# Sign bits' products moved to even turns, weights' steps spread over five, row sums six wide

## The chip, the cores and the metric

The kernel runs on one core of a Trainium2 chip. The metric is device time in microseconds; three runs of the kernel before gave 622.32 as the median (620.95 to 622.4). Five engines work at once, each through its own instructions in order: TensorE (PE; its weight loads are shown as PEld), VectorE (DVE), ScalarE (ACT), GpSimd (POOL), and SyncE (SP), which here only issues transfers.

## What is computed

Attention in which a query sees only keys of the same hash bucket, then a gated feed-forward layer. The reference, shortened:

```python
q_bits = (einsum('bhsd,dk->bhsk', q, proj) > 0)      # 6 sign bits; the same for k
mask = q_bucket[:, :, :, None] == k_bucket[:, :, None, :]
scores = where(mask, scale * q @ k.T, -1e9)
attn = softmax(scores);  x = attn @ v                # 4 batches, 8 heads, 768 tokens, 64 wide
gate = sigmoid(causal 5-tap convolution of x)        # x: 4 x 768 x 512
out = (gate * (x @ w_val)) @ w_out
```

The weights arrive as float64 and are split into a high and a low float32 part.

## The kernel before, in words

There are 32 heads (`units`), each with six tiles of 128 queries, so 192 turns of one loop over `k` (L514). A pipeline runs through the turns. Turn `k` copies the transposed probabilities of tile k - 4 out of PSUM (ScalarE, L348), takes the row maximum of tile k (VectorE, L297), forms its factor and shift (L303, L307), issues the scores of tile k + 1 (TensorE, L291) and the exponentials of tile k (ScalarE, L315), and ends with the transposes of tile k - 3 (TensorE, L339). On even turns the row sums of two tiles are taken (`row_sums`, L321, and `recip`, L325); GpSimd scales the probabilities by them (L330). On odd turns the product with the values follows (`av`, L362).

Between these, generators are stepped, each step issuing a little work: `preps` makes the next head's stacked operands (copies and a difference on GpSimd, L195 and L198, then transfers on SP, L199 to L207); `convs` the convolution (four of five taps on VectorE, L393); `moes` the feed-forward; `weights` the splitting of the eight weight tiles, of six turns each; `ahead` the sign bits of heads 16 to 31.

**Sign bits.** The mask is made by adding rows to the score matmul: twelve rows of sign bits stand below the 64 rows of each operand. For four heads at once, `bits` (L221) or `early_bits` (L236) multiplies half of their rows by `proj_sb` into one PSUM bank (four small matmuls, called a product below), and VectorE turns it into bits by a comparison (L232, L254). Products and comparisons are issued in one step, one behind the other. The bits of heads 0 to 15 come from `bits`, whose operands `raws` are the heads' whole inputs, five buffers; for heads 4 to 15 it runs at the end of the `prep` of the head before. Those of heads 16 to 31 come from `early_bits`, in turns 9 to 57 with k % 6 equal to 3 or 4; its rows are loaded apart, into the feed-forward's `hh` and `hl` buffers (five each), and the bits are stored to memory (`ud`).

**The bank.** The pool `ps_m` has one bank, `m`. The feed-forward's sums use it from turn 65 on, the products and, in `split_weight` (L105), the weights before that: a weight tile holds it from the absolute value on ScalarE (L111) to the last of the operations on VectorE that read it (L121).

**What sets the order.** On TensorE, VectorE, ScalarE and GpSimd the program's order is the order of execution. SP's queue is ordered by the planner of the framework, which places a transfer when its data and its buffer are ready by its own estimate; the queue is then in order too, and a transfer that waits holds those behind it. Waits are inserted from the tiles' accesses.

Of the kernel before, what the change touches and what calls it, by code (L numbers as in the profile page):

```python
# [8 lines left out]
FP32 = mybir.dt.float32  # L9
FP32R = mybir.dt.float32r  # L10
AF = mybir.ActivationFunctionType
ALU = mybir.AluOpType
# [14 lines left out]
def kernel(  # L27
# [77 lines left out]
    def split_weight(w, hi, lo, fetch):  # L105
        if w.dtype == I32:

            t = ps_m.tile([P, 512], FP32, name="m")
            l, u = w[:, :, 0], w[:, :, 1]
            a, d, ti = u.bitcast(FP32), l.bitcast(FP32), t.bitcast(I32)  # L110
            nc.scalar.activation(out=t, in_=a, func=AF.Abs)  # L111
            yield
            nc.vector.tensor_scalar(out=t, in0=t, scalar1=LEAST, scalar2=None, op0=ALU.max)
            nc.vector.tensor_scalar(out=ti, in0=ti, scalar1=3, scalar2=0x3fffffff,
                                    op0=ALU.logical_shift_left, op1=ALU.bitwise_and)
            yield
            fetch()
            nc.vector.scalar_tensor_tensor(out=u, in0=u, scalar=-2 ** 30, in1=ti,
                                           op0=ALU.bitwise_and, op1=ALU.bitwise_or)
            nc.vector.tensor_scalar(out=ti, in0=u, scalar1=-2 ** 23, scalar2=None, op0=ALU.bitwise_and)  # L120
            nc.vector.scalar_tensor_tensor(out=d, in0=l.bitcast(U32), scalar=2.0 ** -52, in1=t,  # L121
                                           op0=ALU.mult, op1=ALU.mult)
            yield
            nc.vector.tensor_copy(out=hi, in_=a)
            nc.gpsimd.tensor_tensor(out=a, in0=a, in1=hi.bitcast(FP32), op=ALU.subtract)
            nc.gpsimd.tensor_tensor(out=lo, in0=a, in1=d, op=ALU.add)
        else:
            nc.scalar.copy(out=hi, in_=w)
            yield
            yield  # L130
            fetch()
            yield
            nc.gpsimd.tensor_tensor(out=lo, in0=w, in1=hi.bitcast(FP32), op=ALU.subtract)
# [52 lines left out]
    def prep(i):  # L186

        if i >= len(units):
            return
        b, h = units[i]  # L190
        j = h % 4
        load_values(i)
        r = raws[i]
        aq, ak, bq, bk = stacks[i] = [stk.tile([P, S], FP32R, name=nm) for nm in ("aq", "ak", "bq", "bk")]
        nc.gpsimd.tensor_copy(out=aq, in_=r)  # L195
        if i > 1:
            yield
        nc.gpsimd.tensor_tensor(out=bq, in0=r, in1=aq.bitcast(FP32), op=ALU.subtract)  # L198
        nc.sync.dma_start(out=ak[0:D].bitcast(FP32), in_=aq[D:P].bitcast(FP32))  # L199
        nc.sync.dma_start(out=bk[0:D].bitcast(FP32), in_=aq[D:P].bitcast(FP32))  # L200
        nc.sync.dma_start(out=bk[D:P].bitcast(FP32), in_=bq[D:P].bitcast(FP32))
        nc.sync.dma_start(out=bq[D:P].bitcast(FP32), in_=aq[0:D].bitcast(FP32))
        if i == 1:
            yield
        u = cur["u"]
        nc.sync.dma_start(out=aq[D:M].bitcast(FP32), in_=f32(u[32 * j:32 * j + 2 * NB]))
        nc.sync.dma_start(out=ak[D:M].bitcast(FP32), in_=f32(u[32 * j + 2 * NB:32 * j + 4 * NB]))  # L207
        load_raw(i + 5)
        if j == 3 and i + 1 < len(units):
            if i + 1 in early:  # L210
                cur["u"] = early.pop(i + 1)
            else:
                yield
                yield from bits(i + 1)

    def side_tile():
        if not moes:
            return ps_m.tile([P, 512], FP32, name="m")
        return ps_t.tile([P, 512], FP32, name="tp")

    def bits(i):  # L221

        u = stk.tile([P, S], FP32R, name="u", bufs=2)
        for hf in range(2):
            yield
            sl = slice(hf * HS, (hf + 1) * HS)
            z = side_tile()
            for jj in range(4):
                nc.tensor.matmul(out=z[32 * jj:32 * jj + 32, 0:HS], lhsT=proj_sb,  # L229
                                 rhs=raws[i + jj][:, sl], start=True, stop=True,  # L230
                                 tile_position=(0, 32 * jj))
            nc.vector.tensor_scalar(out=u[:, sl], in0=z[:, 0:HS], scalar1=rows_sb[:, 0:1], scalar2=rows_sb[:, 1:2],  # L232
                                    op0=ALU.is_ge, op1=ALU.mult)
        cur["u"] = u

    def early_bits():  # L236

        for i in range(16, len(units), 4):
            u = dram.tile([P, S], FP32, name="ud")
            rows = []  # L240
            for hf, name in enumerate(("hh", "hl")):
                yield
                rows.append([hp.tile([P, HS], FP32R, name=name).bitcast(FP32) for _ in range(4)])
                for jj, t in enumerate(rows[-1]):
                    b, h = units[i + jj]
                    nc.sync.dma_start(out=t, in_=qk[b, h, :, hf * HS:(hf + 1) * HS])
            for hf in range(2):
                yield
                z = ps_m.tile([P, 512], FP32, name="m")
                for jj, t in enumerate(rows[hf]):  # L250
                    nc.tensor.matmul(out=z[32 * jj:32 * jj + 32, 0:HS], lhsT=proj_sb, rhs=t, start=True, stop=True,
                                     tile_position=(0, 32 * jj))
                t = hp.tile([P, HS], FP32, name="ht", bufs=2)
                nc.vector.tensor_scalar(out=t.bitcast(FP32R), in0=z[:, 0:HS], scalar1=rows_sb[:, 0:1],  # L254
                                        scalar2=rows_sb[:, 1:2], op0=ALU.is_ge, op1=ALU.mult)
                nc.sync.dma_start(out=u[:, hf * HS:(hf + 1) * HS], in_=t)
            early[i] = u

    def first_bits():
        yield from bits(0)  # L260
        load_raw(5)

    def first_prep():
# [53 lines left out]


    def row_sums(k):
        sums[k] = small.tile([P, 2, 2], FP32, name="s1")  # L320
        nc.vector.tensor_scalar(out=sums[k][:, :, 0], in0=ps[k][1][:, :, 0], scalar1=1e-9, scalar2=None, op0=ALU.add)  # L321

    def recip(k):
        ri = small.tile([P, 2], FP32, name="ri")
        nc.vector.reciprocal(out=ri, in_=sums.pop(k)[:, :, 0])  # L325
        rcs[k], rcs[k + 1] = ri[:, 0:1], ri[:, 1:2]

    def normalise(k):
# [152 lines left out]
    tiles = [(i, qt) for i in range(len(units)) for qt in range(KB)]  # L481

    raws, stacks, vts, ss, nbs, ps, tps, sums, rcs, nms, gs, cur = {}, {}, {}, {}, {}, {}, {}, {}, {}, {}, {}, {}
    avs, convs, moes, early = [], [], [], {}
    accs = [(ps_m, "m")]

    def step(gens):

        while gens:
            try:  # L490
                return next(gens[0])
            except StopIteration:
                gens.pop(0)
# [7 lines left out]
    with tc.manual_schedule(engines=ENGINES):  # L501
# [9 lines left out]
        step(weights[0])  # L511
        step(weights[1])
        ahead = [early_bits()]
        for k in range(N + LAG + 1):  # L514
            if 0 <= k - LAG - 1:
                keep_transposed(k - LAG - 1)
            pair = k % 2 == 0 and 0 <= k - 2 < N
            if k < N:
                maxima(k)
            if pair:  # L520
                row_sums(k - 2)
            if k < N:
                factors(k)
            if pair:
                recip(k - 2)
            if 0 <= k - 2 < N:
                normalise(k - 2)
            if k < N:
                shifts(k)
            if k + 1 < N:  # L530
                if tiles[k + 1][0] != tiles[k][0]:
                    finish(preps)
                    preps = [prep(tiles[k + 1][0] + 1)]
                scores(k + 1)
            if k < N:
                exponentials(k)
            if k >= 60 or k % 2:
                step(convs)
            if k % 6 in (0, 2, 4, 5) and k > 4:
                step(weights[0])  # L540
            elif k < 6:
                step(weights[1])

            thin = k // 6 % 8 in (7, 0) and k < 186
            for _ in range(3 if cur["gates"] else (1, 0)[k % 2] if thin else 1):
                step(moes)
            cur["gates"] = max(0, cur["gates"] - 1)
            step(preps)
            if 6 <= k < 60 and k % 6 in (3, 4):
                step(ahead)  # L550
            if k % 2:
                step(avs)
                step(avs)
            if 0 <= k - LAG < N:
                transposes(k - LAG)
# [67 lines left out]
```

## Time and profile before

| | |
|---|---|
| median of 3 runs | 622.32 us (620.95 to 622.4) |
| the profiled execution | 621.24 us, span 619.2 us |
| TensorE busy | 585.0 us, 94% of the span |
| VectorE busy | 434.5 us, 70% |
| ScalarE busy | 420.3 us, 68% |
| GpSimd busy | 387.6 us, 63% |
| granted TensorE clock | 0.997 |

Times in the views are microseconds from the start of the span. In a row of the timeline come start, duration, engine, line, operation, out<-in, shapes and count, and in brackets how long the engine was idle before it and what released it. In a row of a stretch come its bounds and length, then busy time and count for each engine that took part, the granted clock, the share of the transfer engines and GB/s. Matmul ends are modelled, so a busy TensorE isn't TensorE at its peak.

### The profile page before, as it was taken

To read this page: it belongs to the slowest core of one execution; us is meant where nothing else is said; L and a number is where in the kernel's file an instruction comes from. 1 tells how busy PE (TensorE), PEld (TensorE's weight loads), DVE (VectorE), ACT (ScalarE), POOL (GpSimd) and SP (SyncE) were. 2 spreads that over 40 slices of the span, in tenths; PEclk is the share of its full clock that TensorE was granted. 3 is DMA by queue.
4 is the path that set the end of the run, shared out by engine and by line. 5 is a ranking of instruction groups with operands and counts; after the bars stand their busy time and mean duration, and the time that the engine had idled before them with its cause. 6 is when DMAs were issued, how large, how long until landed. Compare 5 with 4: busy or idle time off the path is not lost.

```text
span 619.2 us, 10665 instructions
## 1 busy us (share of the span) xinstructions
PE 585.0 (94%) x3496; PEld 421.4 (68%) x3496; DVE 434.5 (70%) x1017; ACT 420.3 (68%) x881; POOL 387.6 (63%) x373
## 2 busy tenths in 40 slices
PE   5799998989899999999999999999999999999997
PEld 2665655556567776776668787777667777775895
DVE  5787889898885866668575867668665877665532
ACT  2786777677778676777787676777787766765400
POOL 3575777677866765578665777468764776544321
PEclk9899999999999999999999999999999999999999
DMA  7575767473533334243434234333422213200111
GB/s 228 167 209 168 216 170 208 129 202 82 132 82 74 79 77 130 73 108 83 125 80 115 55 83 123 87 112 83 108 70 78 68 43 92 66 19 1 51 52 51
DMA packets 29030, 64.64 MB, mean 104 GB/s; under 512 B 4936, under 2 KB 10056, under 8 KB 28976
## 3 DMA queue, kind: packets, MB, share of 16 engines
q1 hardware_dynamic: 28832, 63.93, 37.7%
q8 instruction: 28, 0.46, 0.3%
q14 instruction: 26, 0.21, 0.1%
q10 hardware_dynamic: 144, 0.03, 0.0%
HBM read 30.60 MB, written 7.86 MB: 62 GB/s over the span
## 4 chain that ended last, share of the span: by engine, by line
PE 71%; ACT 14%; DVE 11%; issue 2%; DMA 2%; SPq 0%; POOL 0%; ACTq 0%; DVEq 0%; POOLq 0%
PE av L362 19%; PE s L291 17%; PE tp L339 13%; PE m L449 8%; PE m L424 7%; ACT p L315 6%; ACT pt L348 4%; DVE nm L297 3%; ACT x L370 2%; DVE g L393 2%; PE tp L424 1%; PE tp L449 1%; PE s L449 1%; PE m L229 1%; PE s L424 1%
## 5 line engine op out<-in xcount | busy, mean ns | idle before, releaser
L330 POOL TENSOR_SCALAR p<-p,ri 128x768 f32<-128x768 f32 x192 | 205.0, 1072 | 157.7 <-DVE nb L307 131.3
L297 DVE TENSOR_REDUCE nm<-s 128x1 f32<-128x768 f32 x192 | 182.6, 951 | 63.9 <-PE s L291 63.5
L348 ACT COPY pt<-tp 128x384 f32<-128x384 f32 x384 | 165.7, 485 | 81.7 <-PE tp L339 80.9
L315 ACT ACTIVATE p<-s,nb,gs 128x768 f32<-128x768 f32 x192 | 192.7, 1003 | 40.5 <-DVE nb L307 35.6
L339 PEld LDWEIGHTS tp<-ident,p 128*128 128x128 f32 x1152 | 129.2, 141 | 71.8 <-issue 45.2
L339 PE MATMUL tp<-ident,p 128*128 128x128 f32 x1152 | 163.8, 278 | 2.8 <-ACT pt L348 2.2
L362 PE MATMUL av<-pt,vt 128*64 128x384 f32 x768 | 144.9, 498 | 0.0
L291 PE MATMUL s<-ak,aq 76*128 76x384 f32 x384 | 117.7, 387 | 19.6 <-ACT p L315 16.9
L291 PE MATMUL s<-bk,bq 128*128 128x384 f32 x384 | 100.6, 343 | 0.4 <-DVE bq L277 0.4
L362 PEld LDWEIGHTS av<-pt,vt 128*64 128x64 f32 x768 | 46.9, 136 | 63.0 <-issue 62.9
L291 PEld LDWEIGHTS s<-ak,aq 76*128 76x128 f32 x384 | 59.0, 193 | 35.6 <-ACT p L315 31.8
L393 DVE SCALAR_TENSOR_TENSOR g<-x,cw_sb,g 128x768 f32<-128x768 f32 x64 | 77.3, 1208 | 2.2 <-POOL g L391 2.1
L291 PEld LDWEIGHTS s<-bk,bq 128*128 128x128 f32 x384 | 71.2, 192 | 0.8 <-issue 0.8
L198 POOL TENSOR_TENSOR bq<-r,aq 128x768 fp32r<-128x768 f32 x31 | 57.5, 1853 | 0.1
L435 POOL TENSOR_TENSOR hl<-ht,hh 128x384 fp32r<-128x384 f32 x32 | 32.2, 1006 | 39.4 <-DVE hh L433 39.4
L370 ACT COPY x<-av 64x384 f32<-64x384 f32 x64 | 30.4, 474 | 30.9 <-PE av L362 30.2
L383 POOL TENSOR_TENSOR xl<-x,xh 128x384 fp32r<-128x384 f32 x32 | 33.4, 1059 | 18.0 <-DVE xh L382 18.0
L424 PE MATMUL m<-xh,wv 128*128 128x384 f32 x200 | 42.7, 337 | 0.0
L307 DVE TENSOR_SCALAR nb<-nm,gs 128x1 f32<-128x1 f32 x192 | 40.2, 209 | 3.5
L315 ACT ACTIVATION_READ_ACCUMULATOR p<-s,nb,gs 128x1 f32 x192 | 39.1, 203 | 0.0
L429 DVE TENSOR_TENSOR ht<-m,g 128x384 f32<-128x384 f32 x25 | 13.9, 556 | 35.7 <-PE m L424 29.3
L449 PE MATMUL m<-wo,hh 128*128 128x512 f32 x144 | 38.1, 394 | 0.0
(86 smaller groups left out, 483.7 us busy)
## 6 DMA issues: line engine op xcount, KB each, us to landing
r<-in_qk_dram SPq DMA_DIRECT2D x32, 384.0 KB
vt<-in_v_dram SPq DMA_DIRECT2D x16, 384.0 KB
out_dram<-o SPq DMA_DIRECT2D x24, 256.0 KB
ak<-aq SPq DMA_DIRECT2D x31, 192.0 KB
bk<-aq SPq DMA_DIRECT2D x31, 192.0 KB
bk<-bq SPq DMA_DIRECT2D x31, 192.0 KB
bq<-aq SPq DMA_DIRECT2D x31, 192.0 KB
hh<-in_qk_dram SPq DMA_DIRECT2D x16, 192.0 KB
```

Of the source, the lines that this page charges most:

```text
L198: nc.gpsimd.tensor_tensor(out=bq, in0=r, in1=aq.bitcast(FP32), op=ALU.subtract)
L291: nc.tensor.matmul(out=s[:, hf, 0:HS], lhsT=lq[0:n, qs], rhs=rk[0:n, hf * HS:(hf + 1) * HS], start=n == M, stop=n == P)
L297: nc.vector.tensor_reduce(out=nm, in_=s[:, :, 0:HS], axis=AX.XY, op=ALU.max, negate=True)
L315: nc.scalar.activation(out=p, in_=s[:, :, 0:HS], func=AF.Exp, bias=nb, scale=gs.pop(k), accum_out=sm[:, k % 2, 0:1])
L330: nc.gpsimd.tensor_scalar(out=p, in0=p, scalar1=rcs.pop(k), scalar2=1.0, op0=ALU.mult, op1=ALU.mult)
L339: nc.tensor.transpose(out=tp[:, n * P:(n + 1) * P], in_=p[:, kb * P:(kb + 1) * P], identity=ident)
L348: nc.scalar.copy(out=pt[:, :, qo:qo + P], in_=tp[:, 0:HS].rearrange("p (a b) -> p a b", b=P))
L362: nc.tensor.matmul(out=av[s * D:(s + 1) * D, 0:HS], lhsT=vt[:, kb, hh * D:(hh + 1) * D], rhs=pt[kb // 3][:, kb % 3, :], start=(kb == 0), s ...
L370: nc.scalar.copy(out=x[hh * D:(hh + 1) * D, o:o + HS], in_=av[s * D:(s + 1) * D, 0:HS])
L393: nc.vector.scalar_tensor_tensor(out=g, in0=x[:, k:k + S], scalar=w, in1=g, op0=ALU.mult, op1=ALU.add)
L424: nc.tensor.matmul(out=acc[:, 0:HS], lhsT=wv[wi][:, c, j * P:(j + 1) * P], rhs=xs_[(c, o)][xi], start=(m == 0), stop=(m == 11))
L449: nc.tensor.matmul(out=acc, lhsT=hs[(o, j)][hi][:, tb * P:(tb + 1) * P], rhs=wo[wi][:, j, :], start=(m == 0), stop=(m == 11))
```

## The change

The products get turns written out by hand (`marks`), all even and, up to turn 52, the fifth of six; the comparison (`signs`) follows one turn later, behind that turn's exponentials. All use the bank `m`; `side_tile` goes. `bits` for heads 4, 8 and 12 no longer hangs on `prep` but is a generator of its own. `early_bits` loads both halves of its first group in one step at turn 8, and each half of the next group right behind the comparison of that half. The weights' steps come at the end of a turn, after the products, and in five turns of six (not the fourth); the first of the three operations that followed the fetch (L118) gets a step of its own ahead of it. The row sums are written three times over, as six columns, and the reciprocal reads the first two.

```diff
@@ split_weight
             yield
-            fetch()
             nc.vector.scalar_tensor_tensor(out=u, in0=u, scalar=-2 ** 30, in1=ti,
                                            op0=ALU.bitwise_and, op1=ALU.bitwise_or)
+            yield
+            fetch()
             nc.vector.tensor_scalar(out=ti, in0=u, scalar1=-2 ** 23, scalar2=None, op0=ALU.bitwise_and)
@@ prep
+        if j == 0:
+            cur["u"] = us.pop(i)
         u = cur["u"]
...
         load_raw(i + 5)
-        if j == 3 and i + 1 < len(units):
-            if i + 1 in early:
-                cur["u"] = early.pop(i + 1)
-            else:
-                yield
-                yield from bits(i + 1)
+    def product(rows):
+        z = ps_m.tile([P, 512], FP32, name="m")
+        for jj, t in enumerate(rows):
+            nc.tensor.matmul(out=z[32 * jj:32 * jj + 32, 0:HS], lhsT=proj_sb, rhs=t, start=True, stop=True,
+                             tile_position=(0, 32 * jj))
+        return z
+
+    def signs(out, z):
+        nc.vector.tensor_scalar(out=out, in0=z[:, 0:HS], scalar1=rows_sb[:, 0:1], scalar2=rows_sb[:, 1:2],
+                                op0=ALU.is_ge, op1=ALU.mult)
@@ bits, each half
             yield
-            z = side_tile()
...
+            z = product([raws[i + jj][:, sl] for jj in range(4)])
+            yield
+            signs(u[:, sl], z)
+        us[i] = u
@@ early_bits
+        groups = list(range(16, len(units), 4))
+        rows = [early_rows(16, 0), early_rows(16, 1)]
+        for i in groups:
             u = dram.tile([P, S], FP32, name="ud")
...
             for hf in range(2):
                 yield
+                z = product(rows[hf])
+                yield
                 t = hp.tile([P, HS], FP32, name="ht", bufs=2)
+                signs(t.bitcast(FP32R), z)
                 nc.sync.dma_start(out=u[:, hf * HS:(hf + 1) * HS], in_=t)
+                if i != groups[-1]:
+                    rows[hf] = early_rows(i + 4, hf)
+            us[i] = u
@@ row_sums, recip
-        sums[k] = small.tile([P, 2, 2], FP32, name="s1")
-        nc.vector.tensor_scalar(out=sums[k][:, :, 0], in0=ps[k][1][:, :, 0], scalar1=1e-9, scalar2=None, op0=ALU.add)
+        sums[k] = small.tile([P, 6], FP32, name="s1")
+        nc.vector.tensor_scalar(out=sums[k], in0=ps[k][1][:, :, 0].unsqueeze(1).to_broadcast([P, 3, 2]), scalar1=1e-9,
+                                scalar2=None, op0=ALU.add)
...
-        nc.vector.reciprocal(out=ri, in_=sums.pop(k)[:, :, 0])
+        nc.vector.reciprocal(out=ri, in_=sums.pop(k)[:, 0:2])
@@ the loop
+        near = {i: [bits(i)] for i in (4, 8, 12)}
+        marks = {8: ahead, 10: near[4], 16: near[4], 22: ahead, 28: ahead, 34: near[8], 40: near[8], 46: ahead, 52: ahead,
+                 54: ahead, 56: ahead, 58: near[12], 60: near[12], 62: ahead, 64: ahead}
...
                 exponentials(k)
+            if k - 1 in marks and k > 9:
+                step(marks[k - 1])
             if k >= 60 or k % 2:
                 step(convs)
-            if k % 6 in (0, 2, 4, 5) and k > 4:
-                step(weights[0])
-            elif k < 6:
-                step(weights[1])
...
             step(preps)
-            if 6 <= k < 60 and k % 6 in (3, 4):
-                step(ahead)
+            if k in marks:
+                step(marks[k])
+            if k % 6 != 3 and k > 4:
+                step(weights[0])
+            elif k < 6:
+                step(weights[1])
```

More of the change, by code (lines that the diff above doesn't have):

```diff
@@ L208, in prep @@
         load_raw(i + 5)
-        if j == 3 and i + 1 < len(units):
-            if i + 1 in early:
-                cur["u"] = early.pop(i + 1)
-            else:
-                yield
-                yield from bits(i + 1)
[L216 to L219, printed above, removed]
+    def product(rows):
[7 more added lines that the diff above has]
+                                op0=ALU.is_ge, op1=ALU.mult)
     def bits(i):
@@ L226, in bits @@
             sl = slice(hf * HS, (hf + 1) * HS)
-            z = side_tile()
[L228 to L233, printed above, removed]
@@ L234, in bits, with early_rows @@
-        cur["u"] = u
+            z = product([raws[i + jj][:, sl] for jj in range(4)])
+            yield
+            signs(u[:, sl], z)
+        us[i] = u
+    def early_rows(i, hf):
+        rows = [hp.tile([P, HS], FP32R, name=("hh", "hl")[hf]).bitcast(FP32) for _ in range(4)]
+        for jj, t in enumerate(rows):
+            b, h = units[i + jj]
+            nc.sync.dma_start(out=t, in_=qk[b, h, :, hf * HS:(hf + 1) * HS])
+        return rows
     def early_bits():
-        for i in range(16, len(units), 4):
+        groups = list(range(16, len(units), 4))
+        rows = [early_rows(16, 0), early_rows(16, 1)]
+        for i in groups:
@@ L239, in early_bits @@
             u = dram.tile([P, S], FP32, name="ud")
[L240 to L246, printed above, removed]
             for hf in range(2):
                 yield
[L249 to L252, printed above, removed]
+                z = product(rows[hf])
@@ L253, in early_bits @@
+                yield
                 t = hp.tile([P, HS], FP32, name="ht", bufs=2)
-                nc.vector.tensor_scalar(out=t.bitcast(FP32R), in0=z[:, 0:HS], scalar1=rows_sb[:, 0:1],
-                                        scalar2=rows_sb[:, 1:2], op0=ALU.is_ge, op1=ALU.mult)
+                signs(t.bitcast(FP32R), z)
                 nc.sync.dma_start(out=u[:, hf * HS:(hf + 1) * HS], in_=t)
-            early[i] = u
+                if i != groups[-1]:
+                    rows[hf] = early_rows(i + 4, hf)
@@ L259, in first_bits @@
+            us[i] = u
     def first_bits():
-        yield from bits(0)
+        u = stk.tile([P, S], FP32R, name="u", bufs=2)
+        for hf in range(2):
+            yield
+            sl = slice(hf * HS, (hf + 1) * HS)
+            signs(u[:, sl], product([raws[jj][:, sl] for jj in range(4)]))
+        cur["u"] = u
         load_raw(5)
@@ L483 @@
     raws, stacks, vts, ss, nbs, ps, tps, sums, rcs, nms, gs, cur = {}, {}, {}, {}, {}, {}, {}, {}, {}, {}, {}, {}
-    avs, convs, moes, early = [], [], [], {}
+    avs, convs, moes, us = [], [], [], {}
     accs = [(ps_m, "m")]
@@ L513 @@
         ahead = [early_bits()]
+        near = {i: [bits(i)] for i in (4, 8, 12)}
+        marks = {8: ahead, 10: near[4], 16: near[4], 22: ahead, 28: ahead, 34: near[8], 40: near[8], 46: ahead, 52: ahead,
+                 54: ahead, 56: ahead, 58: near[12], 60: near[12], 62: ahead, 64: ahead}
+        for gens in near.values():
+            step(gens)
         for k in range(N + LAG + 1):
```

## The prediction

> **What bounds the kernel now.** I read the page first, then stretches of the main loop, then the chain of waits and the timeline inside the bad stretches. "Turn k" is one pass of the main loop. A stretch runs from the exponentials of turn 10 to those of turn 16, and so on in sixes, six turns being what one head takes.
>
> The page of the kernel before, its header and the chain by engine:
>
> ```profile
> span 619.2 us, 10665 instructions
> PE 71%; ACT 14%; DVE 11%; issue 2%; DMA 2%; SPq 0%; POOL 0%; ACTq 0%; DVEq 0%; POOLq 0%
> ```
>
> TensorE ends most waits of the whole run. The change touches only turns 0 to 65, so these have to be read alone. Busy time by stretch, of the instructions that touch `proj_sb` (the sign bits' products; a product is 4 matmuls, shown as 8):
>
> ```profile
> 36.00:52.99 16.99, 1.71 (x16) 0.32 (x16) 0.00 (x0) 1.00 0.66 196
> 52.99:69.50 16.51, 1.71 (x16) 0.31 (x16) 0.00 (x0) 1.00 0.71 206
> 69.50:84.50 15.00, 0.00 (x0) 0.00 (x0) 0.00 (x0) 1.00 0.60 170
> 84.50:102.14 17.64, 1.71 (x16) 0.32 (x16) 0.00 (x0) 1.00 0.71 200
> 102.14:119.12 16.98, 1.71 (x16) 0.32 (x16) 0.00 (x0) 1.00 0.51 143
> 119.12:137.19 18.07, 1.70 (x16) 0.31 (x16) 0.00 (x0) 1.00 0.70 196
> 137.19:152.15 14.96, 0.00 (x0) 0.00 (x0) 0.00 (x0) 1.00 0.38 99
> 152.15:169.09 16.94, 1.71 (x16) 0.32 (x16) 0.00 (x0) 1.00 0.48 123
> 169.09:184.85 15.76, 1.71 (x16) 0.32 (x16) 0.00 (x0) 1.00 0.32 81
> ```
>
> This table carries the forecast. I number its rows 1 to 9. Rows 3 and 7 hold no product, though a whole weight tile is split in each, and take 15.00 and 14.96, mean **14.98**. The six rows 1, 2, 4, 5, 6 and 8 hold two products each and take 103.13 together, 17.19 each. So a product costs (17.19 - 14.98) / 2 = **1.10 us** as placed now. What it needs on TensorE alone, and what it does to VectorE, is in turn 28 (timeline):
>
> ```profile
> 84.68 0.85 PE L251 MATMUL m<-hh,proj_sb 128*32 128x384 f32 x8
> 85.47 0.87 PE L339 MATMUL tp<-ident,p 128*128 128x128 f32 x6
> 85.68 0.68 DVE L254 TENSOR_SCALAR ht<-m,packed 128x384 fp32r<-128x384 f32 x1 [1.64 <-PE m L251]
> ```
>
> The next work starts 0.79 us after the product. The comparison that reads it is queued on VectorE in the same turn: VectorE sits idle 1.64 us with the next maximum behind it. The chain of waits goes through that place and stays on VectorE up to turn 34:
>
> ```profile
> 85.68 0.68 DVE ht L254
> 86.36 0.87 DVE nm L297
> 101.33 0.41 DVE s L321
> 102.14 0.99 ACT p L315
> ```
>
> In turn 14 two waits stand in a row: the product for the bank `m`, which the weights hold until L121, then VectorE for the product.
>
> ```profile
> 46.39 0.69 DVE L121 SCALAR_TENSOR_TENSOR w<-w,m 128x512 f32<-128x512 uint32 x1
> 47.14 0.85 PE L229 MATMUL m<-r,proj_sb 128*32 128x384 f32 x8 [1.23 <-DVE w L121]
> 48.09 0.68 DVE L232 TENSOR_SCALAR u<-m,packed 128x384 fp32r<-128x384 f32 x1 [1.00 <-PE m L229]
> ```
>
> **The change part by part.** Products leave turns 14, 15, 16, 21, 28, 33, 38, 39, 40, 45, 52, 57, 62 and 63 and go to 10, 16, 22, 28, 34, 40, 46, 52, 54, 56, 58, 60, 62 and 64. All these are even, so no `av` matmuls stand behind them in their turn. Rows 1, 2, 3, 4, 5, 6 and 7 then hold one each, rows 8 and 9 three each, and the last comes after row 9.
>
> *Price of a product in its new place.* The bank is free there: the weights let go of it two turns earlier. So is the reader's wait. What remains is TensorE's own time less the idle that it fills. How much idle there is, in turns 22 and 34:
>
> ```profile
> 69.59 0.82 PE L339 MATMUL tp<-ident,p 128*128 128x128 f32 x6
> 70.66 0.62 PE L291 MATMUL s<-ak,aq 76*128 76x384 f32 x2 [0.25 <-ACT p L315]
> 103.28 0.61 PE L291 MATMUL s<-ak,aq 76*128 76x384 f32 x2 [1.00 <-ACT p L315]
> ```
>
> The 1.00 follows a stretch in which VectorE was late, so it should shrink; 0.25 is the undisturbed value. Price 0.79 - 0.25 = **0.54**, between 0 (a whole 1.00 idle is there) and 0.79 (no idle at all). I take 0.54, because rows 3 and 7 are the state that the others should come to. If the idle goes, each product costs 0.25 more.
>
> *The comparison, a slot behind* (0.68, the rows L232 and L254). It runs after the shifts of an odd turn, its product long done, so nothing on VectorE waits for TensorE. Behind it are the convolution step and the next maximum. The next weights' absolute value on ScalarE writes the same bank and now waits for the comparison, but it stands behind an exponential of 0.99 (the row L315) that starts when the comparison does: cost 0, at most 0.68 if that cover went.
>
> VectorE's own load is the check on the sum. Busy time of all engines (PE, PE loads, DVE, ACT, POOL) in rows 3, 4 and 6, then that of L321 alone in rows 4 and 6:
>
> ```profile
> 69.50:84.50 15.00, 13.93 (x86) 9.16 (x84) 13.11 (x31) 12.46 (x28) 11.52 (x13) 1.00 0.60 170
> 84.50:102.14 17.64, 16.28 (x108) 10.08 (x106) 16.14 (x37) 12.79 (x28) 13.14 (x13) 1.00 0.71 200
> 119.12:137.19 18.07, 16.30 (x108) 10.09 (x106) 16.83 (x38) 12.78 (x29) 13.79 (x13) 1.00 0.70 196
> 84.50:102.14 17.64, 0.80 (x3) 1.00 0.71 200
> 119.12:137.19 18.07, 1.43 (x3) 1.00 0.70 196
> ```
>
> *Row sums.* Each now writes six columns. As it stands it takes far longer than its work at times:
>
> ```profile
> L321 DVE TENSOR_SCALAR s<-sm x96: 150/160/808, 17.6 to 561.9; 128x2 f32<-128x2 f32 x96
> L303 DVE TENSOR_SCALAR gs<-nm 128x1 f32<-128x1 f32 x192 | 29.1, 151 | 3.3
> 109.84 0.91 POOL L330 TENSOR_SCALAR p<-p,ri 128x768 f32<-128x768 f32 x1
> 109.97 0.79 DVE L321 TENSOR_SCALAR s<-sm 128x2 f32<-128x2 f32 x1
> ```
>
> It ends 0.01 us after the GpSimd instruction that began before it: the pair of columns waits for GpSimd. The same operation on one column, L303, has a mean of 0.151 over 192 and so never waits. Six columns are bounded by these two, 0.15 and 0.81; I take 0.16, the median of L321 itself, since the waiting goes with the pair. Off the chain that is worth nothing; rows 4 and 6 are where VectorE ends the waits. There its busy time becomes 16.14 - 0.68 - (0.80 - 0.48) = 15.14 and 16.83 - 0.68 - (1.43 - 0.48) = 15.20: one comparison less, three row sums at 0.16. The fullest that VectorE gets in these rows is 16.83 / 18.07 = 0.93, so these two stretches can't be shorter than 16.3 each.
>
> [...]
>
> *The weights' steps.* L118 moves from the third turn of a tile's six to the second. The five operations on VectorE and the fetch's turn stay. The step now stands behind the convolution step and the products; 0, within the load just counted.
>
> *The row loads on SP.* The 32 loads and 8 stores stay. Eight loads are issued at turn 8 instead of four at 10 and four at 15, and a group's next loads right behind its comparison. 0 by choice; a rival below takes the other end.
>
> *Head.* The convolution weights' steps move behind the first comparison:
>
> ```profile
> 15.11 0.17 DVE L93 TENSOR_SCALAR cwt<-cwt 128x20 f32<-128x20 f32 x1
> 15.31 0.18 DVE L94 TENSOR_SCALAR cwt<-cwt 128x20 int32<-128x20 int32 x1
> 16.17 0.68 DVE L232 TENSOR_SCALAR u<-m,packed 128x384 fp32r<-128x384 f32 x1 [0.68 <-PE m L229]
> ```
>
> They now fill VectorE's idle ahead of it and would then stand behind it: +0.3, between 0 and 0.35.
>
> **Sum.** Rows 1, 2, 3, 5, 7: 14.98 + 0.54 = 15.52 each, 77.60. Rows 4 and 6: 16.3 each, 32.6. Row 8: 14.98 + 3 x 0.54 = 16.60. Row 9 has no weights and keeps its own base: 15.76 - 2 x 1.10 + 3 x 0.54 = 15.18. Together 141.98 against 148.85, -6.87. Turn 64 adds 0.54 and the head 0.3: **-6.0**. The profiled execution took 621.24 (span 619.2 and 2.0 around it), which gives 615.2. The median shown, 622.32, lies 1.08 above it, the lowest run 0.29 below. I forecast **615.5**.
>
> **The rivals.**
>
> *The place doesn't matter.* Each product goes on costing 1.10, because VectorE, at 0.87 of row 3 without any, is what ends last, and the comparisons only move. Rows 1, 3, 5, 7 and 2: 16.08 each, 80.4; rows 4 and 6 lose one product, 16.54 and 16.97; row 8 18.28; row 9 16.86. 149.05, +0.2, with turn 64 and the head +1.6: 622.8, within 0.3%. For it: VectorE's chain over the whole of row 4. Against it: that chain begins behind a 1.64 wait that goes.
>
> *The row sums go on waiting* (the change doesn't do what it says there). Rows 4 and 6 become (15.14 + 0.32) / 0.93 = 16.6 and (15.20 + 0.95) / 0.93 = 17.4: +1.4, 616.9.
>
> *The products vanish in idle.* Price 0, and rows 4 and 6 come down to 15.2: 8 x 15.0 + 13.6 = 133.6 with the rest, -15 before the head, some 606.5. With rows 4 and 6 at 16.3 it is 608.7.
>
> *Rows come late, and it gets slower.* The product of turn 56 needs the second half of its group, loaded into buffers that the product of turn 52 frees. SP takes its issues in one order, and around that turn it holds these:
>
> ```profile
> 160.84 0.46 SPq L201 DMA_DIRECT2D bk<-bq  x1
> 164.05 0.59 SPq L173 DMA_DIRECT2D r<-in_qk_dram  x1
> 4.19 0.83 ACT L271 CAST aq<-r 64x768 fp32r<-64x768 f32 x1 [1.73 <-DMA r<-in_qk_dram]
> 163.25 0.96 DVE L297 TENSOR_REDUCE nm<-s 128x1 f32<-128x768 f32 x1 [0.31 <-PE s L291]
> ```
>
> If the four loads stand behind that load of `r`, they are issued, at some 0.5 each, from 164.6 to 166.5 and land some 3.4 us later, as the first load did (issued at 0.74, waited for until 4.19), at 169.9. TensorE would come to the product when the scores of that turn end, about 163.3: a wait of 6.6, with every transpose and score behind it. One such wait eats the gain (621.8); turn 64 meeting the same makes 628. It decides from 7.9 us of such waits in all. Against it: the buffers are free from turn 52, and SP has gaps between 153.99 and 157.76.
>
> **How the numbers follow.** About 0.3%, 1.9 us, is what a measurement here can tell from no change. Forecast (a gain of 3 to 9 us, its own range 612 to 618.5) 0.59; row sums still waiting 0.10 and products vanishing 0.09, both faster; place doesn't matter 0.10, the same; late rows 0.12, of which 0.10 slower. Faster 0.78, the same 0.12, slower 0.10. The range 610 to 621.5 takes in the price bounds from 0.79 (618.5) down to some 0.1, the second rival and the near edges of the other three.
>
> **What would show it.** Right: VectorE idle before L232 and its fellow near 0, products after turn 8 without a wait for L121, rows 1, 2 and 5 near 15.5, row 3 and 7 half a microsecond longer, L321 at 0.16 throughout. Wrong: TensorE waiting for a DMA of `hh`, `hl` or `r` at a product; rows 1, 2 and 5 above 16.5; stretches past turn 66 changed by more than a microsecond in all, for which the sum has no term.

## The result, and the profile after

Six runs of the changed kernel gave a median of **615.41 us** (613.04 to 617.77); six of the kernel before, on the same chip, 621.39 (619.89 to 622.4). The ratio is 0.9906 with a 95% interval of 0.9879 to 0.9934. The kernel is faster, by more than the 0.3% that the prediction took for what a measurement can tell. The forecast was 615.5. The profiled execution took 615.35 us, with a span of 613.2.

The page of the changed kernel, its header and the chain by engine:

```profile
span 613.2 us, 10666 instructions
...
PE 78%; ACT 14%; DVE 2%; DMA 2%; issue 2%; SPq 1%; POOL 0%; ACTq 0%; DVEq 0%
```

VectorE has gone from 11% of the chain to 2%, and TensorE from 71% to 78%. What left the chain shows in the groups of instructions: the comparisons of both kernels (for each row: count, then busy time and mean ns, then the idle time of VectorE just before them and what ended it). Before:

```profile
L232 DVE TENSOR_SCALAR u<-m,packed 128x384 fp32r<-128x384 f32 x8 | 5.4, 676 | 5.0 <-PE m L229 5.0
...
L254 DVE TENSOR_SCALAR ht<-m,packed 128x384 fp32r<-128x384 f32 x8 | 5.4, 675 | 6.2 <-PE m L251 6.2
...
L321 DVE TENSOR_SCALAR s<-sm 128x2 f32<-128x2 f32 x96 | 22.9, 238 | 6.8 <-ACT p L315 6.2
```

After, with the row sums too:

```profile
L222 DVE TENSOR_SCALAR u<-m,packed 128x384 fp32r<-128x384 f32 x8 | 5.4, 672 | 1.3 <-PE m L217 1.3
L222 DVE TENSOR_SCALAR ht<-m,packed 128x384 fp32r<-128x384 f32 x8 | 5.4, 669 | 0.0
...
L327 DVE TENSOR_SCALAR s<-sm 128x6 f32<-128x6 f32 x96 | 14.5, 151 | 5.7 <-ACT p L321 5.3
```

11.2 us of waiting for products are now 1.3, all of it one wait in the head, where the first comparison still stands right behind its product. A row sum takes 0.151 on average instead of 0.238. Turn 28 shows how the comparison is reached now (timeline after; the product starts at 85.24):

```profile
85.24 0.85 PE L217 MATMUL m<-hl,proj_sb 128*32 128x384 f32 x8
...
85.34 0.96 DVE L303 TENSOR_REDUCE nm<-s 128x1 f32<-128x768 f32 x1 [1.23 <-PE s L297]
...
86.66 0.67 DVE L222 TENSOR_SCALAR ht<-m,packed 128x384 fp32r<-128x384 f32 x1
```

The maximum now stands ahead of the comparison, and the comparison starts without any idle time before it.

The prediction's nine stretches again, in the changed kernel (all engines: PE, PE loads, DVE, ACT, POOL; then granted clock, share of the transfer engines, GB/s):

```profile
34.89:54.22 19.33, 16.34 (x94) 9.98 (x92) 12.28 (x31) 12.47 (x29) 11.02 (x13) 0.91 0.65 193
54.22:69.64 15.42, 14.60 (x94) 9.28 (x92) 12.83 (x33) 12.42 (x29) 12.38 (x13) 1.00 0.54 141
69.64:85.05 15.41, 14.59 (x94) 9.29 (x92) 13.21 (x32) 12.43 (x28) 11.37 (x13) 1.00 0.64 181
85.05:100.60 15.55, 14.74 (x94) 9.29 (x92) 14.98 (x36) 12.71 (x28) 12.22 (x11) 1.00 0.70 200
100.60:115.91 15.31, 14.51 (x93) 9.28 (x92) 13.76 (x33) 12.38 (x28) 12.99 (x15) 1.00 0.46 123
115.91:131.46 15.55, 14.73 (x94) 9.28 (x92) 14.98 (x36) 12.71 (x29) 12.23 (x11) 1.00 0.51 140
131.46:146.74 15.28, 14.47 (x93) 9.28 (x92) 13.74 (x33) 12.38 (x27) 12.98 (x15) 1.00 0.58 148
146.74:162.60 15.86, 15.86 (x110) 9.51 (x108) 13.54 (x32) 11.94 (x27) 11.74 (x11) 1.00 0.70 192
162.60:178.43 15.83, 15.83 (x110) 9.50 (x108) 13.40 (x31) 11.97 (x27) 11.41 (x12) 1.00 0.61 169
```

| row | turns | before | predicted | after |
|---|---|---|---|---|
| 1 | 10 to 16 | 16.99 | 15.52 | **19.33** |
| 2, 3, 5, 7 | | 63.45 | 62.08 | 61.42 |
| 4 and 6 | | 35.71 | 32.60 | 31.10 |
| 8 | 52 to 58 | 16.94 | 16.60 | 15.86 |
| 9 | 58 to 64 | 15.76 | 15.18 | 15.83 |
| sum | | 148.85 | 141.98 | 143.54 |

The sum comes out 5.3 below before, where 6.9 had been forecast. Row 1 has grown by 2.3 where it should have shrunk by 1.5, at a granted clock of 0.91. Rows 4 and 6 shrank more than forecast. Outside the table the way from the exponentials of turn 0 to those of turn 10 is 1.4 shorter (22.74 against 24.11), where +0.3 had been forecast. So the right total hides errors of opposite signs, and the experiments had first to find what happened in row 1.

What stands on its critical path? The chain of waits after, in that stretch:

```profile
35.38 0.43 SPq L240
...
35.85 5.26 DMA w<-in_w_val_dram
...
41.20 0.41 ACT m L111
```

A weight tile is late. It is the second one, and its place on SP's queue has changed. SP's issues in the timeline, before:

```profile
19.91 0.43 SPq L158 DMA_DIRECT2D w<-in_w_val_dram  x1
...
32.75 2.10 SPq L246 DMA_DIRECT2D hh<-in_qk_dram  x4
```

After, where the new eight row loads of turn 8 stand ahead of it in program order:

```profile
22.30 0.51 SPq L240 DMA_DIRECT2D hh<-in_qk_dram  x1
24.91 0.58 SPq L240 DMA_DIRECT2D hh<-in_qk_dram  x1
31.32 2.59 SPq L240 DMA_DIRECT2D hh<-in_qk_dram  x2
33.95 1.85 SPq L240 DMA_DIRECT2D hl<-in_qk_dram  x4
35.85 0.43 SPq L160 DMA_DIRECT2D w<-in_w_val_dram  x1
```

The fetch went from 19.91 to 35.85. ScalarE's absolute value of that tile then waits, and all that stands behind it (timeline after):

```profile
41.20 0.63 ACT L111 ACTIVATE m<-w 128x512 f32<-128x512 f32 x1 [2.91 <-DMA w<-in_w_val_dram]
...
42.38 0.84 PE L346 MATMUL tp<-ident,p 128*128 128x128 f32 x6 [1.99 <-ACT pt L355]
...
45.23 2.37 PE L369 MATMUL av<-pt,vt 128*64 128x384 f32 x8
```

The copies out of PSUM (L355) come behind the waiting instruction on ScalarE, and TensorE waits 1.99 for them. Then it runs slowly: the product with the values takes 2.37; at full clock it takes 1.51 (a row of the repeat of this kernel, below). The granted clock in that place (stretches after):

```profile
40.40:42.40 2.00, 0.02 (x1) 0.05 (x1) 0.54 (x1) 1.20 (x3) 2.00 (x2) 1.00 0.90 201
43.60:47.00 3.40, 3.35 (x10) 1.90 (x12) 3.17 (x10) 1.83 (x4) 0.17 (x1) 0.50 0.88 226
```

For 3.4 us TensorE is granted half its clock (0.50), which is 1.7 us of work lost. With the wait of 2.0 that makes 3.7, near the 3.81 by which row 1 missed its forecast. Before the drop TensorE stood idle for 1.99 at one time, and in the 3.41 us up to it, at a granted clock of 1.00, it was busy for 1.07 (stretch after):

```profile
40.17:43.58 3.41, 1.07 (x8) 0.63 (x6) 1.69 (x3) 2.38 (x6) 2.85 (x4) 1.00 0.65 147
```

### The profile page after: what moved, and what is told of

Same layout as the page of the kernel before. It is cut to its first block, busy times and chain, and to the rows that moved or that the text cites. A ratio compares the mean times of both kernels' runs of the same rounds, so it can differ in the third digit from the quotient of the medians.

```text
span 613.2 us, 10666 instructions
## 1 busy us (share of the span) xinstructions
PE 584.1 (95%) x3496; PEld 421.2 (69%) x3496; DVE 426.5 (70%) x1017; ACT 420.2 (69%) x881; POOL 386.8 (63%) x373
## 4 chain that ended last, share of the span: by engine, by line
PE 78%; ACT 14%; DVE 2%; DMA 2%; issue 2%; SPq 1%; POOL 0%; ACTq 0%; DVEq 0%
PE av L369 22%; PE s L297 19%; PE tp L346 15%; PE m L456 8%; PE m L431 7%; ACT p L321 6%; ACT pt L355 5%; ACT x L377 3%; PE m L217 2%; PE tp L431 1%; PE tp L456 1%; PE s L456 1%; PE s L431 1%; DMA w<-in_w_val_dram 1%; SPq L240 1%
## 5 line engine op out<-in xcount | busy, mean ns | idle before, releaser
L355 ACT COPY pt<-tp 128x384 f32<-128x384 f32 x384 | 165.9, 485 | 84.6 <-PE tp L346 83.7
L400 DVE SCALAR_TENSOR_TENSOR g<-x,cw_sb,g 128x768 f32<-128x768 f32 x64 | 75.9, 1186 | 2.2 <-POOL g L398 2.1
```

The costliest lines, as they stand in the source:

```text
L355: nc.scalar.copy(out=pt[:, :, qo:qo + P], in_=tp[:, 0:HS].rearrange("p (a b) -> p a b", b=P))
L400: nc.vector.scalar_tensor_tensor(out=g, in0=x[:, k:k + S], scalar=w, in1=g, op0=ALU.mult, op1=ALU.add)
```

## The experiments

"x1" below is the base of the others: the changed kernel with this one wait taken away. In each edit, lines of the changed kernel are the ones taken out, if nothing else is said.

### Taking the late tile away, twice, and the unchanged kernel again

The first step of `ahead`, which issues the eight loads, moves one turn on, from the products' place in turn 8 to that in turn 9, and so behind the fetch of turn 8:

```diff
-        marks = {8: ahead, 10: near[4], 16: near[4], ...
+        marks = {9: ahead, 10: near[4], 16: near[4], ...
-            if k - 1 in marks and k > 9:
+            if k - 1 in marks and k > 10:
```

> The changed kernel with one edit: the first step of early_bits (eight row loads) comes at turn 9 in place of 8, behind the fetch of the second weight tile in program order. In the changed kernel that tile's load stood behind the row loads on SP, was issued at 35.85 and landed 5.3 us later; ScalarE waited 2.91 us for it and turns 10 to 16 took 19.33 us. Theory (the order on SP makes the tile late): the wait goes, turns 10 to 16 take 15.5 (as turns 16 to 22 do, 15.42), the whole 3.9 us less than the changed kernel, about 611.5. Rival (the transfer engines are full there, 0.88 of them busy from 38 to 40 us, whatever the order): another transfer is late in its place, turns 10 to 16 stay above 18, about 615.

Measured: 613.49 us (610.87 to 613.54), 0.9867 of before [0.9847 to 0.9887]. Row 1 of x1 is 15.42 instead of 19.33, and its clock is full (stretch of this run):

```profile
34.80:50.21 15.41, 14.61 (x94) 9.30 (x92) 12.30 (x31) 12.39 (x28) 11.05 (x13) 1.00 0.75 211
```

The fetch goes out at 22.22, ahead of the rows (SP's issues in the timeline of this run):

```profile
22.22 0.51 SPq L160 DMA_DIRECT2D w<-in_w_val_dram  x1
...
31.30 2.64 SPq L240 DMA_DIRECT2D hh<-in_qk_dram  x4
```

Nothing else has changed by more than 0.1 in any stretch of turns 10 to 66. So the order on SP is shown to be what lengthened row 1. Whether the late tile belongs to the kernel or to that one execution was open, and both kernels ran again together, unchanged.

> The changed kernel once more, beside c2 on the same chip, since the first runs of x1_rows_later fell into two groups 2.3 us apart (611.0 and 613.5) and those of the changed kernel spread over 4.7 us. Theory (the second weight tile comes late in every execution, by the order on SP): ScalarE waits 2 to 3 us for it in the trace again, turns 10 to 16 take 18 us or more, and the times lie 3 to 4.5 us above c2. Rival (that wait was an accident of one execution): turns 10 to 16 near 15.5, the times within 1 us of c2.

> x1_rows_later once more, beside c1 on the same chip. Theory: 3 to 4.5 us below c1, turns 10 to 16 at 15.4; the first ten turns differ from execution to execution by 1 to 3 us with the clock that TensorE is granted there, in both kernels alike. Rival: within 1 us of c1.

Measured: the changed kernel 613.68 (612.28 to 616.29, ratio 0.9882 [0.9861 to 0.9902]), x1 612.11 (610.67 to 613.4, ratio 0.9848 [0.9829 to 0.9868]). The changed kernel's second profile has the late tile again, but a smaller loss (timeline, then the stretch with the product that comes after it):

```profile
35.35 0.43 SPq L160 DMA_DIRECT2D w<-in_w_val_dram  x1
...
40.44 0.63 ACT L111 ACTIVATE m<-w 128x512 f32<-128x512 f32 x1 [1.66 <-DMA w<-in_w_val_dram]
...
41.62 0.85 PE L346 MATMUL tp<-ident,p 128*128 128x128 f32 x6 [0.74 <-ACT pt L355]
...
43.78 1.51 PE L369 MATMUL av<-pt,vt 128*64 128x384 f32 x8
```

```profile
44.00:47.00 3.00, 2.86 (x19) 1.63 (x16) 2.97 (x9) 2.63 (x6) 1.18 (x2) 1.00 0.82 231
```

The issue is as late as the first time (35.35), so that belongs to the kernel. TensorE waits only 0.74, the clock stays full, and row 1 takes 16.53: 1.1 lost, not 3.9. Neither expectation was met: row 1 stayed below 18 and above 15.5, and the two kernels lie 1.6 apart, not 3 or more and not within 1. So the place is a property of the kernel, and the cost differs with the execution: here by how long TensorE stands idle and whether the clock then drops. The granted clocks of the other runs fit that: averaged over the run, the clock was 0.992 in five of the twelve of the changed kernel, which took 615.12 to 617.77, and never under 0.994 in the nine of x1; where those five lost it isn't known. What makes that idle time longer or shorter wasn't tried. The medians put x1 ahead by 1.9 and 1.6 us, but the intervals of the ratios still touch (0.9847 to 0.9887 beside 0.9879 to 0.9934, and 0.9829 to 0.9868 beside 0.9861 to 0.9902). That x1 beats the changed kernel is likely; that both beat the kernel before is certain by these runs.

### The row sums alone, and all but the row sums

The kernel before with `row_sums` and `recip` of the changed kernel:

> The kernel before with the six-column row sums alone. Theory (the gain comes from the waits at the products): the row sums no longer wait for GpSimd (0.15 each, 8 us less VectorE time), but only the stretches where VectorE ends the waits gain: 84.50 to 102.14 and 119.12 to 137.19 by 0.3 and 1.0, and the rest by 1 at most; 0.5 to 2 us less than before, about 620. Rival (the row sums bring most of it): 4 us or more, 617 or less.

```diff
-        sums[k] = small.tile([P, 2, 2], FP32, name="s1")
-        nc.vector.tensor_scalar(out=sums[k][:, :, 0], in0=ps[k][1][:, :, 0], ...
+        sums[k] = small.tile([P, 6], FP32, name="s1")
+        nc.vector.tensor_scalar(out=sums[k], in0=ps[k][1][:, :, 0].unsqueeze(1).to_broadcast([P, 3, 2]), ...
```

Measured: 618.56 us (616.36 to 618.86), ratio 0.9959 [0.994 to 0.9978]. Alone they are worth some 2.4 us in the medians and 3.0 in the nine rows (145.86). This gain was placed at rows 4 and 6 alone in the prediction; there it is 0.5 and 0.7. Row 1 gains 0.65, row 5 0.64 and row 8 0.44 as well, so the row sums' waits stood on the path in more rows than VectorE's fullest.

The same edit the other way round in x1:

> As x1_rows_later, with the row sums of two columns from the kernel before. Theory: 0.5 to 1.5 us more than x1_rows_later, nearly all of it in turns 28 to 34 and 40 to 46. Rival (the row sums bring most of the gain): 4 us more or above.

Measured: 613.24 us (612.03 to 614.85), ratio 0.9877 [0.9854 to 0.99], beside 613.49 for x1: no difference in the medians. In the trace rows 4 to 7 take 62.53 instead of 61.66, so 0.9 us. The row sums in this run's groups, and in the changed kernel the view of the line alone (count, then least, median and greatest ns, first and last start):

```profile
L327 DVE TENSOR_SCALAR s<-sm 128x2 f32<-128x2 f32 x96 | 23.5, 245 | 6.1 <-ACT p L321 5.7
```

```profile
L327 DVE TENSOR_SCALAR s<-sm x96: 141/149/163, 17.0 to 555.8; 128x6 f32<-128x6 f32 x96
```

Two columns go on taking longer at times when the products have moved (mean 0.245, the longest 0.907), and six columns do so in none of 96 cases: the longest is 0.163. That GpSimd is what the two columns wait for shows in the row sums that start with more than 0.3 us of a GpSimd instruction still to run: the kernel before has 12 of them, of 0.33 to 0.81, and the changed kernel 12 as well, of 0.15 at most. Why six columns don't wait isn't shown. But the waits matter little once the comparisons no longer hold VectorE up. Over the nine rows, 148.85 before become 145.86 with the row sums alone, 140.46 with all but them, and 139.62 in x1 with both. The gains of 3.0 and 8.4 come to 9.2 together and not to 11.4: 2.2 of it both remove.

### The comparison back in the product's turn

x1 with each product where it is now, but its comparison right behind it:

```diff
-            if k - 1 in marks and k > 9:
-                step(marks[k - 1])
             if k in marks:
                 step(marks[k])
+                if k > 9:
+                    step(marks[k])
```

> As x1_rows_later, but each comparison is issued in the turn of its product, right behind it, at the same even turns. Theory (the reader's wait is most of what a product cost before): VectorE waits for the products again, 1.0 to 1.6 us each as in the kernel before at turns 14, 16 and 28, a product costs about 1.1 in place of 0.44, and 14 of them make 8 to 10 us: about 620.5. Rival (the even turn and the free bank are what counts): 0 to 2 us, 612 to 613.5.

Measured: 624.1 us (623.57 to 625.12), ratio 1.0055 [1.004 to 1.0071]: slower than the kernel before, and 10.6 above x1. The waits of this kernel (total us, times, longest):

```profile
DVE u L222 <- PE m L217: 12.5, 6, 2.9
DVE ht L222 <- PE m L217: 11.0, 7, 2.5
```

23.5 us of waiting on VectorE, twice what the kernel before had, in 13 waits of up to 2.9 each, and the next maximum stands behind each, in most of them after one step of the weights. Rows 1 to 3, 5, 7 and 8 get 0.6 to 0.9 longer than in x1, row 9 1.8; rows 4 and 6 get 3.3 longer, to 18.86 and 18.80, and there the clock falls too. Row 4 and the place in it where TensorE runs dry:

```profile
83.35:102.21 18.86, 16.51 (x94) 9.91 (x92) 16.30 (x36) 12.70 (x28) 13.26 (x12) 0.91 0.55 169
...
95.00:97.00 2.00, 0.58 (x6) 0.34 (x4) 1.97 (x8) 1.19 (x3) 1.26 (x2) 1.00 0.99 384
97.00:99.00 2.00, 2.00 (x8) 1.04 (x10) 1.93 (x5) 1.21 (x3) 0.53 (x1) 0.76 0.76 211
99.00:102.21 3.21, 3.21 (x16) 1.97 (x12) 2.11 (x8) 1.33 (x4) 2.59 (x3) 0.62 0.04 13
```

TensorE is busy for 0.58 of 2 us, VectorE for 1.97; then the granted clock is 0.76 and 0.62. So the even turns alone are worth less than nothing. The reader a turn behind is what makes them pay.

### Doubling the product, doubling the comparison

Which engine sets the pace of these turns now? x1 with every product computed twice:

```diff
-        for jj, t in enumerate(rows):
+        for jj, t in enumerate(rows + rows):
+            jj %= 4
```

> As x1_rows_later, with every product of the sign bits computed twice into the same bank (128 more matmul rows in the trace; the result is the same). It asks whether TensorE is what ends last in turns 10 to 65. Theory (a product costs TensorE's time less the idle of 0.25 that it fills, and the first product has used that idle up): each second product costs its whole 0.66 to 0.79, stretches with one product go from 15.4 to 16.1, those with three from 15.85 to 18, 10 to 12.5 us in all over x1_rows_later. Rival (VectorE or the round trip through ScalarE ends last): under 4 us.

x1 with every comparison taken twice:

```diff
-        nc.vector.tensor_scalar(out=out, in0=z[:, 0:HS], ...
+        for _ in range(2):
+            nc.vector.tensor_scalar(out=out, in0=z[:, 0:HS], ...
```

> As x1_rows_later, with every comparison on VectorE done twice. Theory (VectorE is off the path once its waits are gone): 0 to 2 us over x1_rows_later, all of it in turns 28 to 34 and 40 to 46, where VectorE is busy for 14.98 of 15.55 us. Rival (VectorE's load sets the pace of these turns): 0.67 for each, 10 us.

Measured, one time each: 621.89 and 616.53 us; in turns 10 to 66, 8.8 us and 2.5 us above x1. Row 2 with two products, beside which the changed kernel's row 2 above has TensorE busy for 14.60:

```profile
52.64:68.72 16.08, 15.25 (x102) 9.56 (x100) 12.88 (x33) 12.36 (x28) 12.39 (x13) 1.00 0.48 138
```

The second product adds 0.65 of TensorE's work and 0.65 of time, and 0.61 each in rows 8 and 9: nothing of it is hidden. A second comparison (0.68) adds nothing in rows 1, 2 and 3, 0.6 and 1.0 in rows 4 and 6, where VectorE is fullest, takes 0.3 back in each of rows 5 and 7, and adds 0.5 and 0.8 in rows 8 and 9. The second product, though, lengthens rows 4 and 6 as well, by 0.62 and 0.64, and rows 5 and 7 by 0.66 and 0.64. Row 4 with two products, then with two comparisons (15.57 in x1):

```profile
84.78:100.97 16.19, 15.37 (x102) 9.53 (x100) 15.48 (x36) 12.67 (x28) 12.24 (x11) 1.00 0.70 190
...
83.84:100.04 16.20, 15.19 (x102) 9.49 (x100) 15.60 (x37) 12.69 (x29) 12.23 (x11) 1.00 0.68 196
```

So TensorE alone sets the pace in rows 1 to 3. Rows 4 to 7 together get 2.6 longer by four second products (2.6 of work) and 1.0 by four second comparisons (2.7 of work): TensorE's work counts there in full, and in rows 4 and 6 VectorE has no room either. Rows 8 and 9 have room for neither.

### Odd turns

x1 with the marks one turn earlier each (9, 15, 21, 27, and so on to 63), where `av` follows:

```diff
-        marks = {9: ahead, 10: near[4], 16: near[4], 22: ahead, 28: ahead, ...
+        marks = {9: near[4], 15: near[4], 21: ahead, 27: ahead, ...
+            if k == 8:
+                step(ahead)
```

> The changed kernel with the products one turn earlier each, in odd turns, where the matmuls with the values follow in the same turn, the comparisons still a slot behind; the first row loads behind the weights' fetch as in x1_rows_later. Theory (the price is TensorE's time less the idle of its turn, and an odd turn has none): 0.79 in place of 0.44 for each product, 4 to 6 us more than x1_rows_later. Rival (only the wait of the reader and the bank counted): within 1 us of x1_rows_later.

Measured: 618.53 us (616.73 to 618.83), ratio 0.9952 [0.9935 to 0.9968]; turns 10 to 66 are 5.0 longer than in x1. A row with one product takes 15.76 to 15.79. Above the 14.98 of a row without a product that is 0.80, the 0.79 that a product needs on TensorE, with no idle time filled. In even turns it is 15.42 - 14.98 = 0.44. So an even turn hides 0.35 of a product. The comparisons have moved along, to even turns, but none of them waits for its product there, and x6 found no cost of a comparison in rows 1 to 3.

### Four steps of the weights' work

x1 with L118 and the fetch in one step again:

```diff
-            yield
-            fetch()
...
-            if k % 6 != 3 and k > 4:
+            if k % 6 in (0, 2, 4, 5) and k > 4:
```

> As x1_rows_later, with the weights in four steps of six turns as before (L118's operation together with the two that follow it), still behind the products. Theory (the spreading is worth nothing): within 0.5 us of x1_rows_later. Rival (the forecast had turns 28 to 34 and 40 to 46 at 16.3 and they took 15.55, and the spreading is why): 1 to 2 us more, in these two stretches.

Measured: 613.52 us (613.23 to 614.19), ratio 0.9871 [0.9856 to 0.9886], beside 613.49 for x1. Rows 4 and 6 are 0.3 longer, rows 5 and 7 0.27 shorter: the fifth step moves a little work between neighbours. Row 9 is 0.9 longer, and the waits of this run (total us, times, longest) show why; the timeline has the place:

```profile
PEld m L215 <- DMA r<-in_qk_dram: 0.8, 1, 0.8
```

```profile
159.72 1.76 PE L215 MATMUL m<-r,proj_sb 128*32 128x384 f32 x8
```

Its 4 matmuls take 1.76 instead of 0.85. A product that waits for its rows is the rival "rows come late", in small.

## Why the prediction was right, point by point

**The mechanism** held. "It runs after the shifts of an odd turn, its product long done, so nothing on VectorE waits for TensorE": the wait is 0.0 in all eight comparisons L222 of the heads 16 to 31, and undoing this one step costs 10.6 us (x4). The rival "the place doesn't matter" (622.8) fell twice: by the rows after, and by x6, where a second comparison in rows 1 to 3 costs nothing.

**The price of a product** was 0.54, out of 0.79 - 0.25. Measured: the mean of rows 2 to 7 after is 15.42, 0.44 above 14.98. The idle time that a product fills is 0.35; 0.25 had been read from one score. The two ends were sound: x7 found the upper one, 0.80, and the rival in which products vanish in idle time, at a price of 0, fell.

**Rows 4 and 6.** "The fullest that VectorE gets in these rows is 16.83 / 18.07 = 0.93, so these two stretches can't be shorter than 16.3 each" failed. They took 15.55, with VectorE busy for 14.98, a share of 0.963. The ratio had been taken from stretches in which VectorE itself waited for products, and so it was no ceiling. That VectorE has no room there is so (x6), but it doesn't decide alone: a second product lengthens these rows by 0.62 and 0.64 (x5).

**Rows 8 and 9.** Row 8 was forecast at 16.60 and took 15.86, row 9 at 15.18 and took 15.83. Both seem to have one cause: TensorE is busy for all of them, 15.86 of 15.86 and 15.83 of 15.83. Three products at some 0.65 of its work on top of the 13.93 of a row without any make 15.9. In row 8 the first 1.05 of that work filled the idle time of the base (14.98 less 13.93), so three products cost 0.29 each. In row 9 "keeps its own base: 15.76 - 2 x 1.10" gave 13.56, below TensorE's own 13.93: 1.10 was the price in other rows, and here the removed products can't have cost that much. This is argued, not run: x5 agrees, with 0.61 for each second product in both rows, but second comparisons lengthen these rows too (x6), so TensorE's work may not be the whole of it.

**The row loads on SP**, "0 by choice", is the step that failed by the most. Row 1 was forecast at 15.52 and took 19.33 in one profile and 16.53 in the next; a row 1 above 16.5 was among the prediction's own signs of being wrong. The rival "rows come late" named the right queue and the wrong victim: it followed the new loads to their own reader and didn't ask which old transfer they were moved past. Its bound was 6.6 for one such wait; the measured loss was 1.1 to 3.9.

**Row sums.** 0.16 was right (0.151, at most 0.163), and the rival in which they go on waiting fell. That they matter in rows 4 and 6 only was wrong for the kernel before (x2: gains in rows 1, 5 and 8), and of small weight after (x3: 0.9 in the trace, nothing in the medians).

**The head** was forecast at +0.3 and came out at -1.4. Neither can be told: x1 and its repeat are the same kernel, and take 22.75 and 24.58 over the same turns. The moved weights' steps cost nothing that could be measured (x8), and past turn 66 the changed kernel differs from before by 0.3 us, nearly all of it in turns 120 to 132 (35.91 against 35.62); its cause wasn't looked for.

**The sum.** Row 1 is 3.8 above its term, the other rows together 2.2 below theirs, the head 1.7 below its own, and turn 64 0.4 (2.30 after 2.14 before, where 0.54 was added). So the forecast was exact by cancellation, which is luck; the direction and the size of the main gain, rows 2 to 8, rest on a mechanism that held. Without the late tile (x1) the medians are 613.49 and 612.11, 2.0 and 3.4 below the forecast.

## What to carry to other kernels

Where an in-order engine reads the result of another, queue the reader a slot behind and the work that others wait for ahead of it: here that alone decided between 1.3% faster and 0.5% slower than before. When transfers are moved forward on an ordered queue, list the older transfers that they now stand ahead of, and cost those readers (here one, 1.1 to 3.9 us); the loads' own reader is the easy half. Before taking a stretch's price from an average over others, compare the result with the bottleneck engine's own work in that stretch: it can't come out below (row 9 was put at 13.56 without its products, where TensorE alone has 13.93).

## What was unexpected of the hardware

A single idle time of TensorE of 1.99 us was followed by 3.4 us at a granted clock of 0.50, which nearly doubled its cost; one of 0.74 at the same place was not (1.00). A drop came in rows 4 and 6 of x4 too (a mean granted clock of 0.91 in each row), behind a longest idle time of 1.42 each; in x6 one of 1.49, after row 9, was followed by none: the eight matmuls behind it took 1.64, and in the changed kernel eight like them took 1.63 at a clock of 1.00. Row 4 of x4, then x6 (timeline):

```profile
96.95 0.62 PE L297 MATMUL s<-ak,aq 76*128 76x384 f32 x2 [1.42 <-ACT p L321]
...
183.03 1.64 PE L432 MATMUL m<-xh,wv 128*128 128x384 f32 x8 [1.49 <-DVE ht L223]
```

So the length of the idle time alone doesn't tell whether the clock drops; what does wasn't tried.

The first ten turns of one and the same kernel took 22.75 and 24.58 us in two executions, and 22.7 to 25.8 over all kernels that were run here. The granted clock over these turns was 0.80 in the longest and 0.92 in the shortest; but x2 took 24.47 at a clock of 1.00, so the clock doesn't explain all of it. Changes of a microsecond can't be read from that part of a single profile.
